# Linformer attention and MLP-mixer on one core: the first batch's loads in another order, and a new written-out order for the opening

## The chip, the cores and the metric

The kernel runs on one core of a Trainium2 chip. The core has a matrix engine (TensorE, "PE" in the profile, with "PEld" for its weight loads), a vector engine (VectorE, "DVE"), a scalar engine (ScalarE, "ACT"), GpSimd ("POOL") and SyncE ("SP"). Each works through its own queue of instructions in order and waits on semaphores for the others. Data is moved by 16 DMA engines, which are fed from queues on SP, ACT and POOL. Matmul results land in PSUM, which has eight banks. The metric is the device time of the whole program in microseconds, the median over runs.

## The reference, cut to what matters

Eight batches; eight heads of 64; a sequence of 1024. First an attention with projected keys and values, then a mixer over tokens and channels:

```python
k_proj = np.einsum('ks,bhsd->bhkd', E, k)          # 1024 -> 64
v_proj = np.einsum('ks,bhsd->bhkd', F, v)
attn = softmax(q @ k_proj.T / 8);  x = attn @ v_proj    # heads side by side: x is (B, 1024, 512)
u = x + (relu(x.T @ w_tok1) @ w_tok2).T            # over tokens, 1024 -> 256 -> 1024
out = u + relu(u @ w_ch1) @ w_ch2                  # over channels, 512 -> 1536 -> 512
```

## The kernel before, in words

The matmuls run in bf16, and the casts from float32 are made by the loads. Batch 0 is a lead-in of its own, the "opening"; from batch 1 on, the attention of the next batch is woven into the channel matmuls of the present one, so that the matrix engine always has channel work (`up_set`, L1180, and `down_block`, L1289, both in a seven-product Strassen form) beside the short attention steps.

In the opening the eight heads are handled as four pairs, 0 to 3 (pair g holds heads 2g and 2g+1). The first batch's q, k and v come as twelve loads of two heads each (`load_heads`, L358), 512 KB in float32 and 256 KB as written. Per pair the steps are:

- `kv_proj` (PE, L521): 16 matmuls that project k and v together. Pair 3 is handled apart: k first, v later, 8 matmuls each. Copies to `kb` and `vb` follow, on ACT or DVE (L334, L336).
- `k_transpose` (PE, L574, one matmul) and a copy to `kT`.
- `q_transpose_pe` (PE, L618, 8 transposes) and a copy of 1024 columns to `qT`.
- `scores` (PE, L637, 4 matmuls into two banks), then two exponentials on ACT (L652) into `a`.
- `attend` (PE, L672): four units of two matmuls; each is followed on DVE by a reciprocal (L686) and a multiplication into `x_sb` (L692), the normalisation.

After that come `token1_part` (PE, L1060: 16 units of four matmuls, which need x of a pair and token weights wt1, in two half loads), `token2_part` (PE, L1092: eight units of eight matmuls, which need wt2; each is followed by an addition into `u` on DVE, L1105), `u_transpose_pe` (PE, L1121: eight units of four, with copies) and then the first channel products. The channel weights are combined on DVE (L476), as are the sums of u (L807).

E and F are transposed on PE in two halves (L462) and copied to `EFT_sb` by ACT and DVE (L465); every `kv_proj` needs both. Ahead of that PE warms up on zeros (L436), and between the early steps it runs "fills": matmuls of 512 columns on zeros whose result nobody reads.

Nothing is scheduled at run time. `Planner.plan` reads the order of all 2204 jobs from the string `ORDER` (two characters per job, a number in base 64, in the order in which the jobs are created) and the PSUM bank of every job that takes one from `SPOTS`. `FILLS` lists the places in that order at which a fill stands ahead of a PE job, once for every fill. An engine's queue holds its jobs in this order, and the loads stand in POOL's queue in it:

```python
for place, j in enumerate(plan):
    if j.eng == "PE":
        for _ in range(FILLS.count(place)):
            blank(zero)
        pin()
```

`LOADS` names the pieces of the first batch, but the order in which they are issued is that of `ORDER`.

Of the kernel before, what the change touches and what calls it, by code (L numbers as in the profile page):

```python
# [12 lines left out]
ACT = mybir.ActivationFunctionType  # L13
EARLY = 12.0
ORDER = (
    "0R000T0Q090P0S0102040W050U0X030V0A1+061-2007240s080v0w0t0u250x0C0z0+0D0y0-111L0B101M1E0E181G1B151C19"
    "1F0H1A1J261I1K1H1D12271N13140G16171P1O0F1W1c1X1Y1T1g1Q1Z1f1e1R1d1S1j0I1U1V1h1k1a1i281b2N0J291l2S1n2O"
    "2T1m0K2P2Q2A1o1u2U1p2R1v1x1r1q3C211s1t2V1y222X232W2Y1w2E1z2H2B2K2F2I2Z2C2a2L2J2l3B2b2D2h2G332M2i2c0M"
    "2d2e342f2p2m2g0L352x2q362t2y2j0O2r2u2k2n372o0Y2-380N2s2v3L302w2z393M0c3D3v0Z2+313I3N3H323d0a3E3O3J3j"
    "3e0d4c0e3P3A3f3Q0f3h0g3g3R9w3F3i0b3S3K3w3-0h3k3T0i3x4Y3l3U3V3y3z3G3m3W3X4a4d5p3Y4Z3+4e3Z6B0j3p4f403q"  # L20
    "5r4g414u4h425A5s3n4v0k4j3o455B4y464k4w4b434z0l4i445E4l4x4m3a4-4n474o3r5q5C4p4B5D0o4+503t4C9v5F495251"
    "4D5H0p5u4J0q5v535w3b5I0m54485x5y555KA15t3c4G5z0n4H565L4q4K3u576D4A4I5+6F4L6E4M3s6C6H6G6O4N6A6P6Q6160"
    "6I9x6R62696L5-4E6J6S6T4O6f6Z6367646g6h4F686a6M6K654s4Q6bA2660r4R4r6N6c6U4P5S6V4S6W4U6d6e4T6Y6i6o6u6X"
    "6j6l6k5T6m6n6r6x6p5U4V6q6s6y6+6z5G6-4W5a705b4X6t5J74717A72736v5M756w77765N785O585Q7B79595c5X7C5R5Y7J"
    "7H7K7F7I7Q7D7G7S7EA55Z7L7R4t5d5PA6A75eA8AA5VA3A45f5W5h5g7M5i7N5lAD5j7O7V5k7Z7W7X7n7a7Y5m7PA97o7d5n7b"
    "7e7T7p7c7r9z7q7g7s7f7hAF7u7iAH7jAG9-7l7U7v7t7mAJ83AI7wAN7x84AOAhAK7zAi7yALAM877kAjAQ857+88Ak8986AP8A"
    "ARASAbAlAm8BAWAcAdAeAX8D8CATAZ8LAfAgENAaAU8F9y8EAEAVB38MAY8GEO8mB4B5AnAt8iAB8n8+AoAz8k8N8oAC7-8q8pAu"
    "5o8T8H8rAv8U818-8jAq8tA+Ap928JAw90A-93Ar8QAs918lB68uAxB095Ay8K9G96B7B18wB8B28s8xB98R9HBBBD988v9K8S99"
    "9IBEBC94EQBF9+EP8yBGBA8W97BI8zBH9A8V9L8X9BBJ9J9NBK9M829OBL8IBN8YBM9QBOA0BV9RBPBR8aBWBSBTBQBk80BYBl8b"
    "BZBaBXBUBcBb8OBd8P9PBfBnBeBp9SBgBhBmBiERBoBjBq8Z9YES9CET9Z9TEWBr9a8e9E8f9UBs9g8cBu9hBt8dC19WEZBzBwC2"  # L30
    "9dB-BxEVC5EU9iC3C69e8gC4C89V8h9DEbC9EYBv9bEdC0Ec9c9FEfEj9fCBEeEgEkElCC9jEhEiEmByB+9kEn9XEpEr9lC7EqCF"
    "CAEo9nCGEsEtCDCHCEEuCI9o9mCJEvEwExCK9rEyEzCXCMCYE+CLCNE-F0CZ9s9pCaCbCO9qF19tCcCdEXCRF2F3F49uCPF5F6Ce"
    "CQEaCpF7CfILFBCSChIMCgCqCiF9CjFCFACrDEFDDADFDCDSFEF8DGDICkDHFGCTDJFFFHClCxDTCVDLFIFLDBFJFMDUFKFPCnDW"
    "DVFQCyDDDXCmFNDMFTFRDKFOFUDOCzCuDPDNFWCvFXDZCwFiDaFaFVFbDQDcFSFcFYDdC+FZFfDkFgFdC-FeFjIPDRFhDlINCUD0"
# [3 lines left out]
    "J9GMHCJAEHEKJ8GPJBGQHQJCELGnGdJ6GbEMJEGeEIJDJFH8GfHRMJHAJJJGGgGhGRMKJKJHHDH9HUGiJIHSGTHEHVHGGjGlJLHH"  # L38
    "JNJRJMGoHTGSJSHiJOHFHJJPJWGpHXJXHKHIHYHBJUGvJVHaHLHMGUJYHNJTHOJZHbGsJQHjHPGtJaHmJbHnJdJcGwJgGxHkHWJe"
    "MNGmJhJfMLGuHZGkJjMRHpHlJkHcHqHoMOGyHrMPJlHdMQJnMSHsMMJoHuHtGzHvGqG+JiHwGrJpH0JmJzG-H1J+HeH+H2J-HyH3"  # L40
    "JqJvH-JrMVJsI0JxH4JtMTK0K1HxH5K2MXH6I6MaHgMbKBHhI7MZJwMYJyK4I8KCI3K5MfMcMgI4MhK7MdMeJuKDK8I5KFMiHfKG"
    "K3MmI9KEK6KIMkHzMnKJIAMoMpMjK9IBKLMqKAKMKHMrIDKKIEMsKTIFI1KUIGMtMlI2MuMvH7KXICKVMUKYMwKNKWQHMxMyKaKZ"
    "KOKbMzIHM+M-LAN3KlLBL6KdL8N0KcLCN1LEN2LDIILFL9N5N7LON6N8KfKeN4N9LPLHKgNBLIL7KmIJNALSKPKnIKNCKhLKQIKi"
    "NDLGLLNEMWLQKRLTNHLJLRNFNIKtKQNGNLKuKjLgKvNJKSNPLVNQNKKqNMLhKkNUNNLWLMNONVLiNSLkQKQJNTKrLNKoLlNWLYNX"
    "KpLZKsNRLjLnNYLmLoNZKwLpNeNbNfLqNcKxLrNaNhLUNdNjLXQLNiKyNgQONlQMK+NmQNLaKzQPK-QQNnLyLbLsL0L2NkL1LzLt"
    "L3QTL+LcNxLuQRNqLvNyNoO9NtL4M4NvM5OAL5LwLeNzOBM6N-OCNuM1NwN+NpM2O0NrO1M3O2ODNsO3QVOEO4O5QZLfM7O6O7QX"
    "OGQWO8M8OHLdOFQYLxQaM9QdL-QbQeOIOJM0QfOKOLQcMBUGOMMCMAUFQlMDQgONMFQjMEQmQhORQnQUMGOSOPQSQoQkP4P8QpQi"
    "QqOTP9OVP6OUOXOOQuOWMHPAOjP7PBMIQvQwOYQrOZPCQsQtQxPDOkOaQ+UHPFQyUIQzOdPGQ-ObR0PMOeOcPIPNOfPeOQOlR5Oh"
    "PQR2POPROrR1PPR3PTR6OoOgPUR4R7PWP5R8OpRAR9RBPSPJRCRFOqOsRGPVRDOtPERERJPYPHRHRNRIOuRORKRLPKPXPZRQPfOv"
    "OiRRRSPiPLRURcPjRVRPUJRWRTRMOwRXUNRZUKPlRYPgRaPmReOyRdPaRbPhPoPcUMPkPpRfPnRhULOzRgUOPwO+PqRiO-RjPxPr"  # L50
    "OmRkPyOnPsRlRmQ2OxQ3PuRnRoP0RpRvPvRqS7Q4RwP1RrRtRxP2P-RyRsP3RzS8RuPbUPR+PdS9UQQ0URS0USQ1SBSASDS1UUSC"
# [8 lines left out]
    "YCYOYRYP"  # L60
)
SPOTS = (
    "1722467307234441203466116170466360762302312744331670103172245374067253415210734175262102125107667450"
    "1520620612306606413423170354767105253604361302764621303237243176464774171176417604252570156254404366"
    "2373521237102235700221317730106123406106503414727325704746701646213666333167646254435756374205316107"
    "3513126156167122221112015160746532017414020057236736457430642470552552655172151277014703436566371016"
    "1004135333425222002277525207405235256117403572635617204"
)
FILLS = (17, 17, 22, 22, 23, 30, 30, 30, 36, 36, 36, 36, 36, 42, 42, 53, 53, 70, 70, 70, 70, 70, 70)
WHOLE = 3  # L70
TWO = 2
T1 = 2
# [115 lines left out]
def kernel(  # L188
# [246 lines left out]
    def blank(z):  # L435
        nc.tensor.matmul(  # L436
            banks[5], z, z[:, None, :].to_broadcast([P, NJ, P]), start=True, stop=True
        )
# [1082 lines left out]
# [4 lines that stand above are left out]
# [40 lines left out]
```

## Time and profile before

| what | value |
|---|---|
| time, median of 3 runs | 418.57 us (417.91 to 418.78) |
| the profiled execution | 419.06 us; its span 417.3 us |
| granted TensorE clock, mean | 0.999 |
| PE busy | 407.7 us, 98% of the span |
| DVE busy | 356.8 us, 85% |
| ACT busy | 221.6 us, 53% |
| DMA | 61.70 MB, mean 148 GB/s |

The 1.76 us between span and time lie around the program. The span counts from the first instruction. The DMA engines are close to full for about the first 75 us: that time holds the weights, the first batch and the loads for the next two.

How the loads of the opening stand before, by slot (the place in POOL's queue), with issue and time to landing from the trace:

| slot | before | issued at | landed after | landed at | in this slot in the changed kernel |
|---|---|---|---|---|---|
| 1 | k of pair 0 | 1.27 | 4.5 | 5.8 | q of pair 1 |
| 2 | k of pair 3 | 3.14 | 4.0 | 7.1 | v of pair 1 |
| 3 | v of pair 0 | 3.87 | 5.9 | 9.8 | k of pair 1 |
| 4 | q of pair 0 | 4.58 | 6.5 | 11.1 | q of pair 2 |
| 5 | v of pair 1 | 5.29 | 7.0 | 12.3 | v of pair 2 |
| 6 | q of pair 1 | 6.00 | 7.6 | 13.6 | k of pair 2 |
| 7 | k of pair 1 | 6.71 | 8.2 | 14.9 | v of pair 0 |
| 8 | q of pair 3 | 7.42 | 8.7 | 16.1 | k of pair 0 |
| 9 | k of pair 2 | 8.13 | 9.3 | 17.4 | q of pair 0 |
| 10 | v of pair 2 | 8.85 | 9.9 | 18.7 | k of pair 3 |
| 11 | q of pair 2 | 10.10 | 10.6 | 20.7 | q of pair 3 |
| 12 | wt1, first half | 11.34 | 10.1 | 21.4 | v of pair 3 |
| 13 | wt1, second half | 12.61 | 10.1 | 22.7 | wt1, first half |
| 14 | v of pair 3 | 13.90 | 10.1 | 24.0 | wt1, second half |
| 15 | wt2 (twice the size) | 15.22 | 11.2 | 26.4 | wt2 |
| 16 to 21 | channel weights w1, six pieces | 16.46 to 22.96 | 11.3 to 11.5 | 27.8 to 34.5 | the same six, in the order of their numbers |

### The profile page before, as it was taken

Reading aid. Unit: us, or ns where it says so; the run is one execution under the profiler, and the core shown is the slowest. Engines: PE = TensorE matmul, PEld = TensorE weight load, DVE = VectorE, ACT = ScalarE, POOL = GpSimd, SP = SyncE. Lnnn points to the kernel's source line nnn. Section 1 sums busy time; section 2 is a strip of 40 time slices with the busy share of each in tenths; the row PEclk is TensorE's granted clock in tenths of the full one; section 3 lists DMA queues with packets and bytes.
Section 4 is the critical chain, followed back from the end, with each engine's and each line's share of the span. In section 5 each row is a group of like instructions: output and inputs, shape, how many; then the busy total and the mean of one; then the engine's idle time right before and its main releaser. Section 6 shows DMA issues by size and latency. Waiting matters only on the chain.

```text
span 417.3 us, 9605 instructions
## 1 busy us (share of the span) xinstructions
PE 407.7 (98%) x3911; PEld 344.6 (83%) x3913; DVE 356.8 (85%) x773; ACT 221.6 (53%) x429; POOL 66.8 (16%) x105
## 2 busy tenths in 40 slices
PE   8999999998999999999999999999999999999995
PEld 4489888687888888989988889888889789988884
DVE  2479899778999999989989898889989899978685
ACT  1658884267536564483654555455644755344340
POOL 8453021012102030101201011023000001010010
PEclk9999999999999999999999999999999999999999
DMA  8999999597998997997958599898984402250134
GB/s 165 206 200 205 207 191 193 154 150 128 202 190 161 158 190 123 198 154 149 210 95 170 106 203 161 155 174 138 226 122 115 101 0 102 52 151 11 43 117 137
DMA packets 93900, 61.70 MB, mean 148 GB/s; under 512 B 59040, under 2 KB 89376, under 8 KB 93856
## 3 DMA queue, kind: packets, MB, share of 16 engines
q0 software_dynamic: 35088, 45.09, 56.0%
q1 hardware_dynamic: 58128, 15.27, 22.1%
q10 hardware_dynamic: 640, 0.72, 0.5%
q8 instruction: 30, 0.49, 0.4%
q14 instruction: 14, 0.11, 0.1%
HBM read 59.24 MB, written 16.78 MB: 182 GB/s over the span
## 4 chain that ended last, share of the span: by engine, by line
PE 82%; DVE 9%; DMA 5%; POOL 1%; issue 1%; SPq 1%; ACT 0%; DVEq 0%; POOLq 0%
PE psum L1289 31%; PE psum L1180 30%; PE psum L991 4%; PE psum L875 4%; PE psum L521 3%; DVE x_sb L692 3%; DMA qT<-q_sb 3%; PE psum L672 3%; DMA k_sb<-in_k_dram 2%; PE psum L637 2%; DVE G L1161 1%; DVE G L1216 1%; PE psum L1092 1%; DVE rdn L686 1%; PE psum L712 1%
## 5 line engine op out<-in xcount | busy, mean ns | idle before, releaser
L1289 PEld LDWEIGHTS <-G 128*128 128x128 bf16 x1356 | 130.0, 98 | 18.0 <-issue 3.1
L1289 PE MATMUL psum<-wc_sb,G 128*128 128x256 bf16 x780 | 101.0, 271 | 0.0
L1180 PEld LDWEIGHTS <-wc_sb 128*128 128x128 bf16 x768 | 73.9, 98 | 9.5 <-issue 1.4
L1289 PE MATMUL psum<-wT,G 128*128 128x256 bf16 x576 | 76.1, 273 | 0.0
L1202 ACT ACTIVATE G<-psum 128x512 bf16<-128x512 f32 x96 | 56.4, 601 | 28.4 <-PE psum L1180 27.8
L1216 DVE TENSOR_TENSOR G<-G 128x512 bf16<-128x512 bf16 (+1 forms) x140 | 68.8, 515 | 0.4
L1180 PEld LDWEIGHTS <-wT 128*128 128x128 bf16 x576 | 55.4, 98 | 8.5 <-issue 1.9
L1180 PE MATMUL psum<-S,wT 128*128 128x256 bf16 x384 | 56.7, 273 | 0.0
L1327 POOL DMA_DIRECT2D out_dram<-o x30 | 16.4, 547 | 250.5 <-DVE o L1336 183.8
L1180 PE MATMUL psum<-S,wc_sb 128*128 128x256 bf16 x384 | 56.3, 273 | 0.0
L1180 PE MATMUL psum<-uT,wc_sb 128*128 128x256 bf16 x384 | 56.1, 273 | 0.0
L692 DVE TENSOR_TENSOR x_sb<-psum,rdn 128x256 bf16<-128x256 f32 (+1 forms) x88 | 46.9, 542 | 2.1
L1336 DVE TENSOR_TENSOR o<-psum,u 128x512 f32<-128x512 f32 x59 | 40.3, 684 | 7.4 <-PE psum L1289 6.5
L1223 ACT COPY psum<-psum 128x512 f32<-128x512 f32 x48 | 27.7, 579 | 27.1 <-PE psum L1180 18.4
L1161 DVE CUSTOM_DVE_ANT_0 G<-psum,ua 128x512 bf16<-128x512 f32 x48 | 32.6, 683 | 7.4 <-ACT ua L1208 4.0
L652 ACT ACTIVATE a<-psum 128x512 bf16<-128x512 f32 x64 | 34.6, 605 | 8.2 <-PE psum L637 8.2
L1208 ACT COPY ub<-psum 128x512 f32<-128x512 f32 x48 | 28.3, 589 | 19.1 <-PE psum L1180 11.3
L1208 ACT COPY ua<-psum 128x512 f32<-128x512 f32 x48 | 28.2, 592 | 17.5 <-PE psum L1180 17.4
L1161 DVE CUSTOM_DVE_ANT_0 G<-psum,ub 128x512 bf16<-128x512 f32 x48 | 32.8, 684 | 2.8 <-PE psum L1180 2.5
L1180 PE MATMUL psum<-uT,wT 128*128 128x256 bf16 x192 | 28.8, 273 | 0.1
L672 PE MATMUL psum<-vb,a 128*128 128x130 bf16 x256 | 25.0, 220 | 0.2
L686 DVE RECIPROCAL rdn<-psum 128x4 f32<-128x4 f32 (+1 forms) x88 | 15.3, 184 | 9.9 <-PE psum L672 9.2
(102 smaller groups left out, 497.8 us busy)
## 6 DMA issues: line engine op xcount, KB each, us to landing
out_dram<-o POOLq DMA_DIRECT2D x30, 512.0 KB, 4.5
v_sb<-in_v_dram POOLq DMA_DIRECT2D x14, 512.0 KB, 8.0
k_sb<-in_k_dram POOLq DMA_DIRECT2D x14, 512.0 KB, 10.2
q_sb<-in_q_dram POOLq DMA_DIRECT2D x14, 512.0 KB, 9.3
wc_sb<-in_moe_w_ch_dram POOLq DMA_DIRECT2D x6, 256.0 KB, 11.4
wc_sb<-in_moe_w_ch_dram POOLq DMA_DIRECT2D x4, 384.0 KB, 14.3
k_sb<-in_k_dram POOLq DMA_DIRECT2D x4, 256.0 KB, 6.4
v_sb<-in_v_dram POOLq DMA_DIRECT2D x4, 256.0 KB, 8.5
```

The lines of the kernel that those rows point to most:

```text
L652: lambda g=g, half=half, bk=bk: nc.scalar.activation(out=a_t[g][:, half], in_=bank(bk), func=ACT.Exp, scale=scale),
L672: nc.tensor.matmul(view()[:, k, c].rearrange("p i d -> p (i d)"), a_t[g][:, c, at : at + P], vb[:, g].rearrange("k i d -> k (i d)"), start ...
L686: lambda: nc.vector.reciprocal(out=rdn, in_=view()[:, :, :, :, D]),
L692: lambda: nc.vector.tensor_tensor(out=x_sb[:, rows, g * P : (g + 1) * P].rearrange("p (n c) (i d) -> p n c i d", c=2, i=2), in0=view()[:, ...
L1161: nc.vector._custom_dve(TENSOR_ADD_SAT, out=out, in0=in0, in1=in1, s0=FMAX, s1=0.0)
L1180: nc.tensor.matmul(t[:, c, :], w1_of(n, dd, 2 * m + c), a_of(j, n, dd), start=(n in (1, 7) and c == 0 and dd == 0), stop=(c == 1 and dd == 1),
L1202: lambda: nc.scalar.activation(out=G[:, n, cs], in_=view(src), func=ACT.Relu),
L1208: 512, lambda: nc.scalar.copy(out=dst, in_=view("y")), writes=[(name, s % 2)],
L1216: 512 * len(both), lambda: f(out=G[:, n, c], in0=G[:, a, c], in1=G[:, b, c]), ps=False,
L1223: 512, lambda: nc.scalar.copy(out=view("y"), in_=view("x")), takes=[bk["y"]],
L1289: nc.tensor.matmul(to, G[:, G_OF[n], cc, t * P : (t + 1) * P], w2_of(n, cc)[:, cut], start=(n in opens and (t == 0 or alone) and cc == 0), ...
L1336: 512, lambda: nc.vector.tensor_add(out=dst, in0=view(src), in1=u_of(sh, dh)),
```

## The change

Three constants differ, `ORDER`, `SPOTS` and `FILLS`; no function does. The diff, cut:

```diff
 ORDER = (
-    "0R000T0Q090P0S0102040W050U0X030V0A1+061-2007240s080v0w0t0u250x0C0z0+0D0y0-111L0B101M1E0E181G1B151C19"
+    "0R050T0Q040P0S0308070U061L0V0W01000X021M091E0A1F1G1I1H1J0B1K1N1j1O0C1P1W1X1Y1c0D1e1f1g1d1k1Q0E1h1Z1i"
...
-FILLS = (17, 17, 22, 22, 23, 30, 30, 30, 36, 36, 36, 36, 36, 42, 42, 53, 53, 70, 70, 70, 70, 70, 70)
+FILLS = (21, 21, 21, 21, 21, 21, 21, 27, 27, 30, 35, 35, 45, 45, 45, 53, 53, 68, 68, 80, 80)
```

Decoded, it does this:

- The loads change places as the last column above shows: pair 1, pair 2, pair 0, pair 3, and only then the token weights. The w1 pieces (and the four w2 pieces further on) go in the order of their numbers.
- PE's first 101 jobs are reordered. Up to the first token products the order is (with n fills as "[n]"; "kv" is `kv_proj`, "kT" and "qT" the transposes of k and q, "S" the scores, "A" one unit of attend, "T" half of the transposes of E and F; the digit is the pair):

```
before: T T [2] k3 [2] kT3 [1] kv0 [3] kT0 qT0 [5] S0 qT1 [2] kv1 A0 A0 A0 [2] kT1 qT3 A0 S1 [6] A1 kv2 A1 A1 A1 qT2 kT2 S3 token1 ... S2 ... A2 ... v3 ... A3
after:  T qT1 T [7] kv1 [2] kT1 [1] S1 qT2 [2] A1 kv2 [3] A1 kT2 A1 [2] kv0 S2 kT0 qT0 A1 [2] k3 S0 kT3 [2] qT3 A0 A0 A0 A0 v3 S3 A2 A2 token1 ... A2 A2 A3 ...
```

- There are 21 fills where there were 23.
- ACT's and DVE's queues follow: in the changed kernel ACT's is kT1, two exponentials of pair 1, four copies of kv2, qT2, two kb copies of pair 0, an exponential of pair 2, two vb copies, kT0, qT0, the other exponential of pair 2, two of pair 0, kT3, qT3, two of pair 3. On DVE the 16 normalisations still stand ahead of the first addition into u, in the new order of the pairs; the sums for w1 and u (L476, L807) are interleaved otherwise behind them, and the first of the sums of the token weights (L830) stands later.
- Behind PE's first 101 jobs, ACT's first 64 and DVE's first 87 (they end among the first channel products of batch 0) each engine's own order of compute jobs is the same as before. Behind that, one load differs: the first half of v for batch 2 moves from ahead of batch 2's q to behind the second half of v. In later batches six results go to another PSUM bank.

## The prediction

> **What bounds the kernel now.** First the page, then the opening in windows, in order of time engine by engine, and in the chain of waits.
>
> ```profile
> PE 407.7 (98%) x3911; PEld 344.6 (83%) x3913; DVE 356.8 (85%) x773; ACT 221.6 (53%) x429; POOL 66.8 (16%) x105
> PEclk9999999999999999999999999999999999999999
> ```
>
> PE works nearly all the time, so the end moves only if PE waits or fills less, and that it does, almost alone, in the opening. The windows (busy us of each engine, clock, DMA share):
>
> ```profile
> 15.00:20.00 5.00, 4.83 (x63) 2.76 (x62) 3.53 (x15) 2.28 (x5) 2.96 (x4) 1.00 1.22 208
> 20.00:25.00 5.00, 4.51 (x67) 3.43 (x62) 2.48 (x11) 4.30 (x10) 2.69 (x4) 1.00 1.15 207
> 25.00:30.00 5.00, 4.95 (x79) 4.56 (x79) 4.89 (x19) 0.77 (x2) 2.33 (x4) 1.00 1.44 198
> 30.00:35.00 5.00, 5.00 (x81) 4.91 (x80) 4.87 (x10) 3.87 (x8) 2.52 (x4) 1.00 1.38 200
> ```
>
> Up to 25 PE's time holds waits and fills (the fills count as busy) and DVE is half idle; the loads set the pace. From 25 on PE and DVE are both full. The rows of PE and DVE around that turn:
>
> ```profile
> 24.88 0.63 PE L521 MATMUL psum<-v_sb,EFT_sb 128*64 128x128 bf16 x8
> 25.45 0.84 PE L1060 MATMUL psum<-x_sb,wt_sb 128*128 128x128 bf16 x12
> 26.34 0.72 PE L672 MATMUL psum<-vb,a 128*128 128x130 bf16 x8
> ...
> 24.50 0.25 DVE L686 RECIPROCAL rdn<-psum 128x4 f32<-128x4 f32 x2 [2.19 <-PE psum L672]
> 27.29 1.40 DVE L692 TENSOR_TENSOR x_sb<-psum,rdn 128x256 bf16<-128x256 f32 x4
> 28.67 3.90 DVE L1105 TENSOR_TENSOR u<-psum,x_sb 128x512 bf16<-128x512 f32 x6
> ```
>
> Pair 3's v, landed at 24.0 in slot 14, is projected at 24.88; its attend is at 26.34, and DVE, idle for 2.19 us before 24.50, normalises pairs 2 and 3 until 28.67. The rest runs without a gap: in the chain the next batch's first projection is "41.72 0.99 PE psum L521 x16". My mark for comparison is 35.01, when all of the opening and two groups of channel products are done. One stall is left later:
>
> ```profile
> PE psum L637 <- DMA qT<-q_sb: 1.2, 1, 1.2
> ```
>
> That one, at 98, hangs on transposes which SP issues after a projection at 79.02, so it moves along with PE.
>
> **The loads.** Every load of the first batch has one size, so I take the landings by slot as they were (5.8, 7.1, 9.8, then about 1.3 apart). The DMA share stays the same, and POOL's queue holds the same number of loads ahead of each slot. Three things follow: all q, k and v are there at 21.4 instead of 24.0; wt1 comes one slot later (22.7 and 24.0); wt2 (26.4) and w1 don't move.
>
> **The new order, walked.** Durations from rows of before: a projection takes 0.57 on PE (14.97 to 15.54); its four copies on ACT 0.98 (10.49 to 11.47); a qT copy 1.01, the next starts after 0.91; from the first score matmul to the first exponential 0.46; two exponentials 1.08; a kT copy 0.27; an attend unit 0.13; a token1 unit 0.225; a token2 unit 0.50 (three from 27.46 to 28.96). Start and warm-up stay, with PE free for T at 5.56.
>
> - Pair 1: T, qT1, T end at 7.4, seven fills at 8.9, and k in slot 3 (9.8) starts kv1 at 9.85: PE idles 1.0. DVE's kb copies end at 11.07, kT at 11.67, S1 is at 11.73, exponentials until 13.27.
> - Pair 2: k (slot 6, 13.6) gives kv2 at 13.68, ACT's copies 14.3 to 15.3, qT2 until 16.3.
> - Pair 0: k (slot 8, 16.1) gives kv0 at 16.2. From here ACT's queue is the path: kb until 17.4, exponential of pair 2, vb until 18.3, kT0, qT0 until 19.5, exponential of pair 2, S0 at 19.6, two exponentials until 21.15, kT3 until 21.4, qT3 until 22.4.
> - Pair 3: q in slot 11 (20.7) is turned by 21.4, before ACT is free; v (21.4) is projected from 21.7. S3 is at 22.5, exponentials from 22.95 to 24.04.
>
> Before, pair 3's exponentials shared ACT's 2.19 us block after 22.35; what held pair 3 back was v. So 2.6 us of earlier data become little here: ACT's queue, not the load, is late next.
>
> **PE's sum.** Before, from 24.88 to the mark: 10.13 us. After, PE is past S3 at 22.83; against before at 24.88 it has v3 done (less 0.57) but 7 more token1 units (7 x 0.225 = 1.58) and 4 more attend units (0.52) to do: 11.66, so the mark at 34.5, 0.5 earlier. In that stretch PE needs wt1 at 23.1 (landed 22.7, 24.0) and wt2 at 27.8 (26.4): covered by 0.4 to 1.4 us; if a load is later than that, it counts in full.
>
> **DVE's sum.** From the first normalisation of pair 0 (21.54), DVE has 12 units and two vb copies (0.50). A unit by itself takes 0.55 (20.73 to 21.28); reciprocals side by side bring it to 0.43 (four in 26.99 to 28.69). With the queue's actual pairs I get the end at 28.15 against 28.67. PE waits for single units on the way (the last four attend units and token1 of pairs 2 and 3), 0.3 in all beyond what before has. So 0.5 less 0.3: the mark is 0.2 to 0.3 earlier, and I take 0.3. Bounds: with every unit at 0.43 DVE ends at 27.2, no wait is left and PE can also win back the 0.5 of waits that before has in this stretch, together 1.1 earlier; with each unit at 0.57 and PE waiting for all of it, 0.3 later.
>
> **The rest.** Two fills fewer are 2 x 0.22 of PE time, at places where PE waits anyway: nothing. Token and channel sums on DVE stay as many. SP's queue is unchanged. The half v of batch 2 used to be issued at 43.02 (landed 60.0) and now stands among the loads at 59.65 to 64.06, of which the last landed at 74.1; with 2.6 us more that is under 77, and its reader starts at 79.02: nothing, and beyond that cover one for one. PE found no gap in front of any of the six results that get other banks: nothing. First users of batch 1's loads at 41.72 had them from 39.6: 2.1 us of cover, enough for 1.1.
>
> **A rule.** The granted clock is 1.00 in every window and a 512-column fill takes 0.22 us. The changed order leaves PE 1.0 idle at 8.9 and about a quarter of 10 to 22.5. [...]
>
> **Sum.** 419.06 of the profiled execution less 0.3 is 418.8; that execution was 0.5 above the median, so the median goes from 418.57 to 418.3. About 0.2% (0.84 us) is what can be told from no change.
>
> **Rivals.**
> 1. Faster: DVE pairs its reciprocals better and PE loses the waits. 0.9 to 1.1 earlier: 417.5. For it: DVE has all attend results of pair 2 early, and idles today before 24.50. Against: the queue's order alternates reciprocals and multiplications.
> 2. Slower: the chain through ACT slips. Pair 0's k sits in slot 8 and the eight jobs behind it on ACT all wait in line; one slot (1.28 us) later there, or as much lost between PE and ACT by in-order waiting, passes whole to qT3, S3 and PE: 1.28 less 0.3 is 1.0, so 419.6. It decides from 0.3 on. For it: ACT has no slack from 16.8 to 24, where before it was busy 2.28 of 5 us in 15 to 20. Against: landings by slot have one cause and didn't depend on the tensor.
> 3. Slower: batch 2's late half v delays the transposes behind 79 and the stall at 98 grows by 1.5: 419.8. Against: 2 us or more of cover.
> 4. Slower: the clock falls once. At half clock the PE work of pair 1's stretch (0.57 + 0.23 + 0.34 + 0.45) takes that much again, 1.6: 419.9. Against: 1.00 throughout, and no gap over 1.0.
>
> **How the numbers follow.** Forecast 0.46, rival 1 0.25, rival 2 0.21, rival 3 0.05, rival 4 0.03. Faster by over 0.2% (below 417.7) is rival 1: 0.25; slower (above 419.4) are 2 to 4: 0.29, less 0.01 for small slips: 0.28; within: 0.47. The range from 417.4 to 419.6 leaves out rivals 3 and 4 and the tails of 1 and 2; the forecast's own is 417.9 to 418.9.
>
> **What would show it.** In the changed trace: kv1 at 9.85; v of pair 3 landed by 21.5; S3 near 22.5 and straight behind qT3's copy; DVE without a gap from 21.5 and at its first addition into u at 28.2; token2's first matmul near 27.8; batch 1's first projection at 41.4; the stall at 98 of the same size; clock 1.00. The prediction is wrong if S3 comes after 23 (rival 2), if additions into u start before 27.5 (rival 1), or if PE has a new gap behind 42.

## The result, and the profile after

| | before | changed |
|---|---|---|
| median of 6 runs each | 418.3 us (417.91 to 418.78) | 419.82 us (419.64 to 421.2) |
| profiled execution | 419.06, span 417.3 | 419.9, span 418.1 |

The ratio is 1.0044 (95% interval 1.0030 to 1.0058): slower, by 1.5 us between the medians, where 0.2% can be told from no change. A second comparison, on another chip and with 12 runs of the changed kernel beside 35 of before, gave 1.0024 (1.0014 to 1.0033), which is 1.1 us between the medians. The forecast was 418.3, 0.3 faster; its range ended at 419.6.

The page of the changed kernel, and then its windows of the opening, in the columns of the prediction:

```profile
PE 406.9 (97%) x3911; PEld 344.5 (82%) x3911; DVE 357.0 (85%) x773; ACT 221.2 (53%) x429; POOL 66.8 (16%) x105
PEclk9999999999999999999999999999999999999998
```

```profile
15.00:20.00 5.00, 4.10 (x50) 2.44 (x49) 1.39 (x6) 4.22 (x12) 2.80 (x4) 1.00 1.24 206
20.00:25.00 5.00, 4.49 (x56) 3.14 (x56) 3.44 (x16) 3.81 (x7) 2.38 (x4) 1.00 1.14 210
25.00:30.00 5.00, 4.92 (x80) 4.55 (x78) 4.60 (x17) 1.05 (x3) 2.23 (x3) 1.00 1.41 195
30.00:35.00 5.00, 5.00 (x81) 4.91 (x79) 4.91 (x10) 3.83 (x8) 2.97 (x4) 1.00 1.39 201
```

PE works less between 15 and 20 (4.10 for 4.83), DVE more between 20 and 25 (3.44 for 2.48), and the clock stays at 1.00. The rows around the turn from waiting to full engines, PE first, then DVE, from the timeline:

```profile
21.47 0.62 PE L618 MATMUL psum<-ident,q_sb 128*128 128x128 bf16 x8 [0.31 <-DMA q_sb<-in_q_dram]
22.48 0.63 PE L521 MATMUL psum<-v_sb,EFT_sb 128*64 128x128 bf16 x8
23.19 0.41 PE L637 MATMUL psum<-qT,kT 64*64 64x512 bf16 x4
...
28.27 0.76 DVE L692 TENSOR_TENSOR x_sb<-psum,rdn 128x256 bf16<-128x256 f32 x2
29.23 1.29 DVE L1105 TENSOR_TENSOR u<-psum,x_sb 128x512 bf16<-128x512 f32 x2 [0.20 <-PE psum L1092]
```

Pair 3's scores come at 23.19 (forecast 22.5), 1.1 us behind the end of a q transpose that waited for its load; the normalisation ends at 29.03 (before 28.69, forecast 28.15), and the first addition into u starts at 29.23 (before 28.67). A group of channel products of batch 1 (L1289) serves as a later mark, from here on "the mark at 87.4"; it is the last that I compare ahead of the stall near 98 us. Its row in before, then in the changed kernel:

```profile
87.20 0.82 PE L1289 MATMUL psum<-wT,G 128*128 128x256 bf16 x6
```

```profile
87.73 0.82 PE L1289 MATMUL psum<-wT,G 128*128 128x256 bf16 x6
```

Against the first trace of before, PE is 0.53 us late at the mark and 0.77 late at its end (413.04 for 412.27), so something is lost twice. One late wait of PE grew, the one near 98 us, which was 1.2 us:

```profile
PE psum L637 <- DMA qT<-q_sb: 1.5, 1, 1.5
```

### The profile page after: what moved, and what is told of

It reads as the page before. It is cut to its first block, busy times and chain, and to the rows that moved or that the text cites. A ratio compares the mean times of both kernels' runs of the same rounds, so it can differ in the third digit from the quotient of the medians.

```text
span 418.1 us, 9597 instructions
## 1 busy us (share of the span) xinstructions
PE 406.9 (97%) x3911; PEld 344.5 (82%) x3911; DVE 357.0 (85%) x773; ACT 221.2 (53%) x429; POOL 66.8 (16%) x105
## 4 chain that ended last, share of the span: by engine, by line
PE 82%; DVE 7%; DMA 6%; POOL 2%; issue 1%; SPq 1%; ACT 0%; POOLq 0%; DVEq 0%
PE psum L1289 31%; PE psum L1180 30%; PE psum L991 4%; PE psum L875 4%; PE psum L521 3%; DMA qT<-q_sb 3%; DMA q_sb<-in_q_dram 3%; DVE x_sb L692 3%; PE psum L672 2%; PE psum L637 2%; DVE G L1216 1%; PE psum L1092 1%; DVE G L1161 1%; PE psum L712 1%; PE psum L1060 1%
## 5 line engine op out<-in xcount | busy, mean ns | idle before, releaser
L1289 PEld LDWEIGHTS <-G 128*128 128x128 bf16 x1356 | 130.0, 98 | 18.0 <-issue 3.1
L1289 PE MATMUL psum<-wc_sb,G 128*128 128x256 bf16 x780 | 101.0, 271 | 0.0
L1289 PE MATMUL psum<-wT,G 128*128 128x256 bf16 x576 | 76.1, 273 | 0.0
## 6 DMA issues: line engine op xcount, KB each, us to landing
wc_sb<-in_moe_w_ch_dram POOLq DMA_DIRECT2D x6, 256.0 KB, 11.6
```

Source lines behind the costliest of these rows:

```text
L1289: nc.tensor.matmul(to, G[:, G_OF[n], cc, t * P : (t + 1) * P], w2_of(n, cc)[:, cut], start=(n in opens and (t == 0 or alone) and cc == 0), ...
```

## The experiments

All landings below are from the issue rows of the traces, PE's times from its matmul rows; the mark is the start of the first matmul of its group. Two sums hold in all 17 traces, whatever the order, and make them easy to compare. The mark comes 58.49 to 58.55 us behind the first addition into u. And PE's end comes 323.83 to 323.96 us behind the mark, plus PE's waits in between (the one near 98 us, and 0.22 us near 101 in two traces). So a difference between two traces is either there by the first addition into u, in the opening, or it arises in these waits.

### Both kernels again, and the half load of batch 2

The first edit moves one job in the order before, the second moves the same job back in the changed order (loads of batch 2 in POOL's queue; v0 is the half with heads 0 to 3, v1 the other half, and so for q and k):

```diff
 # the order before, decoded             # the changed order, decoded
-v0 q0 v1 k1 k0 q1                       -q0 v1 v0 k1 k0 q1
+q0 v1 v0 k1 k0 q1                       +v0 q0 v1 k1 k0 q1
```

> The kernel before, unchanged, as a control and for a second trace of it. The medians of the two kernels lie 1.5 us apart (418.3 and 419.8), their two traces only 0.85 (spans 417.3 and 418.1): the profiled execution of before, 419.06, was 0.76 above its own median. Theory 1 (the trace of before caught a late execution, and the change costs 1.5 us in places that this trace hid): the new span is 416.4 to 416.8, and something in it lies 0.5 us or more earlier than in the first trace. Theory 2 (executions scatter by that much and the change costs about what the traces show, 0.5 in the opening and 0.25 at the stall near 98 us): the new span is again near 417. In the time of other runs: the same within 0.1%.

> The changed kernel, unchanged, on the same chip, as the other control. 1.0036 times before if the first comparison holds (1.5 us; interval 1.003 to 1.006). If the loads of the opening land late by a property of the order, q of pair 3 lands again between 21.3 and 21.5 us and the fourth load at 11.4; if it was an accident of that execution, they land as in the trace of before, at 20.7 and 11.05, and the difference to before shrinks by about 0.5 us.

> The kernel before with one job moved: the first half of v for batch 2 goes from ahead of q of batch 2 to behind the second half of v, where the changed kernel has it. Theory 'stall': the second q transpose of batch 2 lands about 0.25 us later, the stall of the matrix engine near 98 us grows by 0.2 to 0.3, and the time grows by 0.2 to 0.3 us (ratio 1.0005 to 1.0008). Rival 'the half load is inert': 0 and no growth of the stall; then the 0.23 us by which the stall grew came with the later opening. Rival 'queue': a transfer behind it is pushed and the loss is 0.5 or more.

> The changed kernel with that one half load of batch 2 back where the kernel before has it. Theory 'stall': 0.2 to 0.3 us faster than the changed kernel (419.5 for 419.8), with the stall near 98 us back at its size before. Rival 'inert': the same time as the changed kernel.

Measured, on one chip, with before at 418.74 (35 runs): before again 418.68, ratio 1.0005 (0.9994 to 1.0016); changed again 419.88, 1.0024 (1.0014 to 1.0033); before with the half load late 419.03, 1.0004 (0.9993 to 1.0014); changed with it early 419.92, 1.0026 (1.0015 to 1.0036). The half load is inert: neither time moved, and the stall did not go back.

The two controls say more, from their timelines near 98 us, before first, then changed:

```profile
96.78 0.28 PE L672 MATMUL psum<-vb,a 128*128 128x130 bf16 x2
97.81 0.63 PE L637 MATMUL psum<-qT,kT 64*64 64x512 bf16 x8 [0.75 <-DMA qT<-q_sb]
```

```profile
96.77 0.28 PE L672 MATMUL psum<-vb,a 128*128 128x130 bf16 x2
98.45 0.63 PE L637 MATMUL psum<-qT,kT 64*64 64x512 bf16 x8 [1.40 <-DMA qT<-q_sb]
```

PE arrives within 0.01 us of the same time (at the mark, 87.39 and 87.38) and then waits 0.75 in the one and 1.40 in the other, for the second q transpose of batch 2 (a DMA that SP issues). It ends at 411.98 and 412.63: all of PE's 0.65 arises in this one wait. In the chain of work that ended last the transpose is a piece by itself (start and length), 11.93 us in before and 12.64 in changed:

```profile
85.84 11.93 DMA qT<-q_sb
```

```profile
85.76 12.64 DMA qT<-q_sb
```

So the opening's loss in the first pair of traces, 0.53 at the mark, is for the greater part an accident of that execution: the fourth load landed at 11.44 there, at 10.91 and 10.59 in the two new traces of the changed order, and the mark followed (87.73, 87.38, 87.09). The second trace of before has the mark 0.19 later than the first (87.39 for 87.20) and PE's end 0.29 earlier, since its stall is 0.48 shorter. The spans of the controls are 0.8 us apart and their medians 1.2 (0.8 by their ratios to before, 1.0005 and 1.0024); what the one pair of traces doesn't show of that stays open here.

### Take the stall away, and three rivals for the opening and the code

```diff
 # both orders, decoded, POOL's queue; store3 is the third store of batch 0's output
-v(batch 3, first half)  store3  q(batch 3, first half)
+v(batch 3, first half)  q(batch 3, first half)  store3
```

> The kernel before with one store moved: the third store of an output half of batch 0, issued at 86.6 us between the two batches' transfers, goes in the POOL queue behind batch 3's load of q, which can't start before the second q transpose of batch 2 has landed. The store's 128 packets take 1.3 us of all 16 DMA engines, inside the time in which that transpose runs. Theory 'stall' (the scores of pairs 2 and 3 near 98 us wait for that landing alone, 0.7 to 1.2 us in the order before): the landing comes about 1.3 us earlier, the wait nearly vanishes, and the kernel gets 0.7 to 1.1 us faster (ratio 0.9974 to 0.9983). Rival 'opening' (the time is set in the opening, the stall moves along): no gain over 0.2 us.

> The changed kernel with the same store moved. Theory 'stall': its wait near 98 us (1.4 to 1.7 us) vanishes as well, it gets 1.2 to 1.6 us faster than the changed kernel, and its matrix engine ends within 0.35 us of the kernel before with the store moved, because the two openings are equal at 87.4 us in the pair of traces taken on one chip. Ratio to before 0.997 to 0.999. Rival 'opening': it stays 0.6 us or more behind the kernel before with the store moved.

Measured, with before at 418.56 on that chip: before with the store moved 417.9, ratio 0.9986 (0.9977 to 0.9996); changed with the store moved 418.42, 0.9998 (0.9987 to 1.0008), where the changed kernel stands at 1.0024. The second transpose landed 10.5 and 10.7 us behind the issue of batch 3's v, for 12.4 and 13.0, and neither trace has a wait for qT on PE; its ends are 410.85 and 411.54. The stall theory holds in kind: 0.6 us gained in the order before, 1.1 in the new one, each a little less than was expected (0.7 to 1.1 and 1.2 to 1.6). The two ends lie 0.69 apart, where at most 0.35 was expected. Of that 0.49 stood at the mark already (86.94 and 87.43), and 0.22 is a new wait near 101 in the changed order. In these two executions the fourth load landed at 10.43 and 11.13. Whether the opening costs something is open here.

The next edit pads DVE's code ahead of everything else, on the changed kernel:

```diff
+    spare = tile_of([P, 8], BF16, "spare")
+    for _ in range(7):
+        nc.vector.memset(spare, 0.0)
```

> The changed kernel with seven writes of zeros into 8 columns that nobody reads, on DVE ahead of everything else, where DVE is idle. The new opening order needs seven semaphore instructions fewer on DVE (910 instructions for 917), so everything behind it stands seven places earlier in DVE's code; the traces show a code fetch for a queue that is not PE's at 90.1 to 90.5 us in the order before and at 87.3 to 88.0 in the new one, and DMA packets stuck near 91 us for 0.5 to 1.3 us a DMA engine before, 2.9 to 3.1 after. Theory 'code position': the fetch goes back to about 90, the stuck time falls to 1.3 or less, the second q transpose lands at 97.8 to 98.0 instead of 98.4 to 98.8, and the time is 0.5 us or more below the changed kernel. Rival 'code does not matter': landing at 98.4 or later and the time of the changed kernel, 1.0024 times before.

Measured: 1.0026 (1.0015 to 1.0037), landing 13.4 us behind, PE's wait 1.8 us, the code fetch at 87.86, within the range without the padding (87.33 to 87.97). The length of DVE's code makes no difference here.

The third edit of this group takes the copy of pair 0's qT from ACT to DVE (one letter of the string that says which engine makes each copy):

```diff
-SIDES = "AAADADADADDAAAAAAAAADAAAAAAAA"
+SIDES = "AADDADADADDAAAAAAAAADAAAAAAAA"
```

> The changed kernel with the copy of pair 0's transposed q on DVE instead of ACT. The prediction made ACT's queue the path of the opening; the three traces of the new order have the scores of pair 3 exactly 1.76 us behind the landing of q of pair 3 (21.43, 21.07, 20.76 to 23.19, 22.83, 22.52). Theory 'landing': that distance stays at 1.7 to 1.8 us, the first additions into u stay where they were against that landing, and the time stays within 0.2 us of the changed kernel. Rival 'ACT': ACT is 1.0 us of work shorter ahead of the scores of pair 3, the distance falls by 0.3 us or more, and the first channel products come 0.3 us or more earlier.

Measured: 1.0027 (1.0017 to 1.0036) for the changed kernel's 1.0024, so no gain. The rows (ACT, then PE) show why:

```profile
20.56 0.27 ACT L336 CAST kT<-psum 128x128 bf16<-128x128 f32 x1
21.64 1.01 ACT L336 COPY qT<-psum 128x1024 bf16<-128x1024 bf16 x1 [0.81 <-PE psum L618]
...
20.98 0.62 PE L618 MATMUL psum<-ident,q_sb 128*128 128x128 bf16 x8 [0.44 <-DMA q_sb<-in_q_dram]
22.75 0.41 PE L637 MATMUL psum<-qT,kT 64*64 64x512 bf16 x4
```

ACT is free 0.81 us before it can copy pair 3's qT (0.41 in the changed kernel), and the scores stay 1.82 us behind the landing of q of pair 3 (20.93). The load sets them here, not ACT's queue.

### One POOL instruction

The DMA engines also bring code: the pages of both kernels have two queues of the kind "instruction", q8 (30 packets, 0.49 MB) and q14 (14 packets, 0.11 MB). With the store moved, the fetch of q14 that is near 88 or 90 us in the other traces was at neither place (100.13 and 100.42). That pointed at POOL, which is then held up behind batch 3's load. POOL's code has 175 instructions in the order before and 176 in the new one (174 and 175 of them are in the traces): ahead of the first q load of batch 1 stands a semaphore instruction that the order before doesn't have, since the load there has one thing to wait for (a DMA) and here two (a DMA and PE). It stands at 33.84 in the first changed trace; both orders have one ahead of the first v load of batch 1 (24.02 and 24.70), which waits for two as well. The first edit below adds an instruction to the kernel before, behind that same q load (the trace has it at 34.51); the second takes one from the changed kernel, a clearing in the opening that isn't needed. Both diffs are cut:

```diff
         j.fn()
+        if j.n == 205:                      # behind the first q load of batch 1
+            nc.gpsimd.memset(spare, 0.0)
```

```diff
-        make_identity(nc, ident32)
+        nc.gpsimd.affine_select(out=ident32, in_=zero32, compare_op=ALU.not_equal,
+                                fill=1.0, base=0, pattern=[[-1, P]], channel_multiplier=1)
```

> The kernel before with one instruction more on POOL: a write of zeros into 8 columns that nobody reads, behind the last load of k for batch 1, so that POOL's code has 176 instructions as in the changed kernel (one semaphore instruction more) and not 175. In the traces the code fetch that is not PE's comes at 90.1 to 90.5 us in the order before, at 87.3 to 88.0 in the new one, and with the store moved, POOL being held up behind batch 3's load, it is at neither place in either order: so it is POOL's. Padding DVE's code left it at 87.9. Theory 'POOL code': the fetch comes at 87.2 to 88.0, the first q transpose of batch 2 takes 4.6 us for 4.41, packets near 91 us are stuck for 2.8 us or more for 0.6 to 1.4, the second transpose lands 13.0 to 13.4 us behind the issue of batch 3's v for 12.4 to 12.9, and the kernel is 0.4 to 0.7 us slower than before (ratio 1.001 to 1.0017). Rival 'another trait of the new order': fetch at 87.6, but landing and time as before (1.000).

> The changed kernel with one instruction less on POOL: the float identity is made from zeros that DVE has already written, so one clearing of 128x128 goes. POOL's code has 175 instructions as before. The loads behind it may be issued up to 0.2 us earlier. Theory 'POOL code': the fetch is back at 90.1 to 90.5 us, the first q transpose takes 4.41, the second lands 12.4 to 12.9 us behind the issue of batch 3's v, stuck packets 0.6 to 1.4 us, and the time is 0.4 to 0.7 us below the changed kernel: ratio to before 1.000 to 1.0015 for 1.0024. Rival 'another trait': landing 13.0 or more behind, ratio 1.002 or more, less what the earlier loads give.

Measured, with before at 418.82: the kernel before with one instruction more 419.85, ratio 1.0017 (1.0009 to 1.0026); the changed kernel with one less 419.06, 1.0001 (0.9990 to 1.0011). Both times lie in the range that was expected, at its upper and its lower end. Three of the signs do not: with one more, 2.0 us of packets are stuck (see the table) where 2.8 or more was expected; with one less, 0.3 are stuck for 0.6 to 1.4, and the transpose lands 12.0 us behind batch 3's v for 12.4 to 12.9. The chain's piece for the second transpose, before with one more, then changed with one less:

```profile
85.60 12.63 DMA qT<-q_sb
```

```profile
85.71 11.58 DMA qT<-q_sb
```

And the fetch, from the DMA view of two stretches: 87.0 to 88.5 us in the control of the changed kernel and in before with one instruction more (both have it there; the control of before has no such line), and 89.9 to 92.9 in the control of before and in changed with one less (queue, then packets, MB and share of the DMA engines' time):

```profile
q14 instruction: 1, 0.01, 1.3%
```

```profile
q14 instruction: 1, 0.01, 1.3%
```

```profile
q14 instruction: 1, 0.01, 1.9%
```

```profile
q14 instruction: 1, 0.01, 1.6%
```

All traces up to here. "Stuck" is the length of the DMA packets that took over 0.4 us and began between 89.8 and 93.5, summed and divided by the 16 DMA engines (the median packet of a load takes 0.1):

| kernel | POOL's fetch | first q transpose | second lands, behind the issue of batch 3's v | stuck | PE's wait near 98 | mark at 87.4 | PE's end |
|---|---|---|---|---|---|---|---|
| before, first trace | 90.31 | 4.41 | 12.85 | 1.4 | 1.2 | 87.20 | 412.27 |
| before, control | 90.54 | 4.41 | 12.38 | 0.6 | 0.7 | 87.39 | 411.98 |
| before, half load late | 90.15 | 4.41 | 12.69 | 1.3 | 1.1 | 87.24 | 412.14 |
| changed, one POOL instruction less | 90.28 | 4.42 | 12.00 | 0.3 | 0.4 | 87.26 | 411.53 |
| before, one POOL instruction more | 87.41 | 5.07 | 13.07 | 2.0 | 1.4 | 87.15 | 412.48 |
| changed, first trace | 87.97 | 4.58 | 13.09 | 3.1 | 1.5 | 87.73 | 413.04 |
| changed, control | 87.64 | 4.62 | 13.02 | 2.9 | 1.4 | 87.38 | 412.63 |
| changed, half load early | 87.33 | 4.61 | 13.31 | 3.0 | 1.7 | 87.09 | 412.62 |
| changed, DVE padded | 87.86 | 4.63 | 13.38 | 3.4 | 1.8 | 87.59 | 413.20 |
| changed, qT of pair 0 on DVE | 87.50 | 4.62 | 13.15 | 3.3 | 1.5 | 87.24 | 412.62 |
| before, store moved | 100.13 | 4.41 | 10.52 | 1.6 | none | 86.94 | 410.85 |
| changed, store moved | 100.42 | 4.43 | 10.67 | 1.7 | none | 87.43 | 411.54 |

Fetch near 90: 12.0 to 12.9 us to the landing. Fetch near 87.5, while the first transpose is in flight: 13.0 to 13.4, without overlap, and the first transpose takes 0.2 to 0.7 longer. One POOL instruction moves it either way. That the fetch is the link, and not something else that the instruction shifts, is concluded from this match alone. The second edit also issues the loads of the opening 0.18 earlier, but its mark (87.26) isn't early; its gain is in the wait, 0.4 for 1.4 to 1.8. That is less than before's 0.7 to 1.2, so the equal time (1.0001) doesn't say that the changed opening is free. In the other direction the wait accounts for part: 1.4 for 0.7 to 1.2, and PE ends 0.2 to 0.5 later than in the three other traces with this order and the store in its place, while the time is 0.7 longer. How a fetch of 8 KB that lasts 0.31 us does this is not shown: the stuck packets are a sign of it and not the whole of it, since with the store moved 1.6 us are stuck and nobody is late.

### No fills

```diff
-FILLS = (21, 21, 21, 21, 21, 21, 21, 27, 27, 30, 35, 35, 45, 45, 45, 53, 53, 68, 68, 80, 80)
+FILLS = ()
```

> The changed kernel without its 21 fills. Theory 'landing' (the opening goes by the landing of q of pair 3): the scores of pair 3 stay 1.7 to 1.8 us behind that landing, the granted clock stays at 1.00 and the time within 0.3 us of the changed kernel. Rival 'clock' (the prediction's fourth): the matrix engine is idle for about 40% of 9 to 22 us instead of a quarter, the granted clock falls in a window before 25 us, matmuls there take up to twice as long, and the kernel is 1 us or more slower.

Measured (4 runs): 421.83, ratio 1.0063 (1.0047 to 1.0079), 1.6 us above the changed kernel's 1.0024. The rival 'clock' holds. Windows (clock third from the right):

```profile
8.00:12.00 4.00, 1.56 (x23) 0.83 (x23) 1.36 (x5) 0.28 (x2) 2.99 (x5) 0.87 1.09 173
12.00:16.00 4.00, 2.60 (x29) 2.13 (x29) 0.61 (x2) 2.28 (x7) 1.86 (x4) 0.50 1.24 205
16.00:20.00 4.00, 3.78 (x40) 2.76 (x38) 1.21 (x5) 2.76 (x8) 2.25 (x3) 0.50 1.24 205
20.00:24.00 4.00, 3.56 (x40) 2.22 (x38) 2.18 (x9) 3.31 (x6) 1.72 (x3) 0.85 1.15 213
```

The granted clock halves at about 11 and comes back at about 21: by windows of 1 us it is 1.00 up to 10, 0.97 from 10 to 11, 0.50 from 11 to 21, 0.91 from 21 to 22 and 1.00 again from 22. Eight transposes take 1.03 us there for 0.62, and pair 3's scores come at 23.72 though its q had landed at 20.08.

### The opening by itself, and a kernel faster than both

The store moved and POOL's clearing of the float identity dropped, in both orders; and in the order before, a third edit:

```diff
 # the order before, decoded, loads in slots 12 to 14
-wt1(first half) wt1(second half) v3
+v3 wt1(first half) wt1(second half)
```

> The kernel before with the store moved as in the earlier run and the float identity made from the zeros that are there. If the opening goes by the landing of its loads and these are issued 0.1 to 0.2 us earlier, it gains as much over the moved store alone: ratio to before 0.9978 to 0.9986, no wait near 98 us. If POOL's clearing was hidden, the same as the moved store alone, 0.9986.

> The kernel before with the same two edits, beside the last one on one chip. 0.9986 times before, as it was, no wait near 98 us; this is the kernel that the two others of this call are compared with.

> The changed kernel with the store moved and the float identity made from the zeros that are there: the wait near 98 us is gone and POOL's code fetch lies near 100 us, as in the kernel before with the same two edits, so that only the openings differ. Theory 'opening neutral' (the whole loss came through the stall): within 0.1% of that kernel, and its matrix engine within 0.3 us at 87.4 us. Rival 'opening costs half' (the two kernels with the moved store lay 0.12% apart, 0.5 us of which stood at 87.4 us already): 0.4 to 0.6 us behind it, ratio to before 0.9995 to 1.0005.

> The kernel before with the same two edits and one part of the change: v of pair 3 ahead of the two halves of the token weights wt1, so that these stand behind all twelve loads; PE's order stays. In the traces of before the first token product starts 0.9 to 1.4 us behind the landing of wt1's first half in slot 12, which now comes in slot 13, 1.25 us later. Theory 'wt1 bounds': the first token product comes 0.3 to 0.9 us later and the kernel is 0.3 to 0.9 us slower than with the two edits alone. Rival 'hidden' (the normalisation on DVE sets when the additions into u start, and PE catches up): the first channel products come at the same time, and the time is the same within 0.2 us.

Measured: the order before with both edits 418.18, 0.9986 (0.9977 to 0.9995), and on another chip, beside the next two, 418.06, 0.9981 (0.9971 to 0.9991); the changed order with both 418.43, 0.9990 (0.9980 to 1.0001); the order before with both and the token weights behind all twelve loads 418.95, 1.0007 (0.9992 to 1.0023). PE at the mark: 86.39 and 86.70 in the order before, 87.08 in the changed one, 87.97 with the late token weights. None of the four has a wait for qT.

So the changed opening alone is 0.4 us behind (0.9990 to 0.9981), and 0.5 in the pair with the moved store; the intervals overlap in both pairs, and the control pair had 0.0 at the mark. The mean mark over the five traces of each order with the opening's POOL work and copies as they were is 87.18 before and 87.44 changed, 0.26 later, in a spread of 0.45 and 0.64. I leave it at 0 to 0.5. With the 0.65 of the stall in the controls that gives an estimate of 0.65 to 1.15 us for the whole change, beside 0.8 to 1.2 measured there.

The order before with only the token weights moved behind loses 1.1 us. Its first product with them, in the order before with both edits and then with the late token weights:

```profile
21.68 0.40 PE L1063 MATMUL psum<-x_sb,wt_sb 128*128 128x128 bf16 x4
```

```profile
22.95 0.40 PE L1063 MATMUL psum<-x_sb,wt_sb 128*128 128x128 bf16 x4 [0.54 <-DMA wt_sb<-in_moe_w_tok_dram]
```

That is 1.27 later, and the mark moves by the same 1.27. Half of it is the execution (fourth load at 11.28 for 10.61), the rest the wait for the later slot, inside the 0.3 to 0.9 expected. The 0.9 to 1.4 us from landing to first product that the expectation starts from don't hold for the first product: it follows by 0.04 to 0.67 in the five traces of before's opening, so the token weights nearly bind there already. Dropping POOL's clearing issues the loads from slot 2 on 0.18 earlier, and PE ends 0.2 to 0.5 earlier in the traces; the times don't settle whether that is a gain (0.9986 and 0.9981 for 0.9986 in the order before, 0.9990 for 0.9998 in the changed one).

The order before with the store moved is faster than the kernel before by 0.14% (0.14% and 0.19% with POOL's clearing dropped too), and so faster than the changed kernel: the one long wait that PE had behind the opening is gone.

## Why the prediction was wrong, point by point

Two steps failed: a stall that was taken to move along grew, and the 0.3 us that the opening was to gain didn't come. The first is shown; of the second the size stays open.

- **"That one, at 98, hangs on transposes which SP issues after a projection at 79.02, so it moves along with PE."** This step failed. The issue does move along with PE; the time from there to the landing was taken as fixed. Counted from the issue of batch 3's v, it was 13.0 to 13.4 us for 12.4 to 12.9 in every trace of the changed order with the extra POOL instruction and the store in its place. That makes PE's wait 1.40 for 0.75 us, which is all of PE's difference in the pair of controls. Removing one POOL instruction takes the wait to 0.4 and the time to 1.0001.
- **"POOL's queue holds the same number of loads ahead of each slot"** is right, and misses what mattered: its code isn't the same length. I counted the loads in each queue and not the semaphore instructions that come with them.
- **Rival 3** had the right place (the stall at 98 grows), but the wrong cause, and its time, 419.8, is right by luck: the stall grew by 0.2 and 0.65 in the two pairs, not by 1.5. Moving the half load back changed nothing. As "The rest" had it, that load costs nothing.
- **"The loads": "I take the landings by slot as they were".** As a mean, right up to slot 10, where the means of the two orders agree within 0.09; from slot 11 on they don't. The fourth load landed at 11.05, 11.04, 11.06, 10.43 and 10.93 in orders before, at 11.44, 10.91, 10.59, 11.13, 11.02 and 10.82 in changed ones. As single values they scatter by up to 0.85 us between executions of one order, and slot 12's 21.43, on which the walk leaned, was the earliest of its kind (21.75 to 22.12 in the four others). Slot 11, on which pair 3's scores hang, landed at 20.51 to 20.94 in five traces of before's opening (mean 20.74) and at 20.76 to 21.43 in six of the changed one (mean 21.09), though at 20.08 in the one without fills; why it comes later isn't shown. A margin of 0.4 us against a load is none.
- **"The new order, walked": "From here ACT's queue is the path".** Wrong wherever q of pair 3 lands behind 20.7: then the scores are 1.76 to 1.82 us behind that landing in seven traces, with or without 1.0 us of work taken off ACT (20.7 is an estimate: 22.47, the earliest scores of the changed order, less 1.76). With its q at 20.76 they come at 22.52, where I had 22.5. With its q at 20.00 (changed order, both edits) they come at 22.47, no earlier: there the chain runs through the load of k of pair 3, in slot 10, and DVE's copies of it.
- **"DVE's sum"** was 0.35 short: from the scores of pair 3 to the first addition into u it is 6.03 to 6.07 us in seven traces with the copies as in the changed kernel and its fills, for 5.7 in my walk; DVE's alternating reciprocals and multiplications take 0.55 a unit in most of that stretch, where I had 0.43 to 0.57 mixed. With slot 11's 0.35 that is the whole miss: the first addition into u comes at 28.92 in the mean of five traces, for 28.2 forecast and 28.66 in before. The 0.3 of further PE waits that I put on top aren't there, since the mark at 87.4 keeps its distance to that addition in both orders.
- **The forecast of "0.3 earlier"** at the end of the opening, from "PE's sum" and "DVE's sum", is the second step that failed. At the mark the changed order is 0.53 later (first pair), 0.01 earlier (controls), 0.15 earlier (the two with the half load moved), 0.49 later (store moved) and 0.38 later (both edits, on one chip). By the mean it is later, and how much of that is the order and how much the landings of single executions isn't settled. The stall hides it in part: with the mark 0.29 earlier than in the control (half load early) the transpose landed at the same 98.41.
- **"A rule": "The granted clock is 1.00 in every window".** It stayed at 1.00 in the changed kernel too, in every window of its trace up to 50 us. That it would, with no gap over 1.0, was my estimate. The fourth rival's fall is real without the fills: the granted clock is 0.50 from 11 to 21 us, where eight transposes take 1.03 us for 0.62. Ahead of that PE's longest gap was 2.3 us, and between 7 and 11 it was busy for 0.88 of 4 us, where the changed kernel with its fills has 3.41 at 1.00. So the 21 fills are worth 1.6 us, though no result of theirs is used. How long a gap, or how little work, brings the clock down is not shown.

## What to carry to other kernels

Before a late stall is said to move along, look at what else runs while the awaited transfer is in flight: a wait on a DMA need not keep step with the engine that waits (here 0.75 and 1.40 us, with PE at the same place within 0.01). A reordering can also change which instructions need an extra wait, so the code's length changes, and with it the times at which code is fetched (here 176 POOL instructions for 175, and a fetch at 87.64 for 90.54 in the controls); compare the number of instructions of each engine, not only the jobs. And take a second trace of the same kernel before giving a landing to a tenth of a microsecond: the fourth load of the changed order landed between 10.59 and 11.44.

## What the runs showed of the hardware that was not expected

- Code is fetched by the DMA engines all through the run: one queue brings 30 fetches of 16 KB (q8, 18.7 to 399.7 us in the first trace of before), another 14 of 8 KB (q14, 33.2 to 413.7). One POOL instruction more or less, which moves a fetch of 8 KB by 3 us (90.54 to 87.41, 87.64 to 90.28), goes with about 0.2% of the kernel's time (1.0017 for 1.0000 in the order before, 1.0024 for 1.0001 in the new one).
- The first q transpose of batch 2 lands 4.41 us behind its issue (4.6 to 5.1 with the fetch near 87.5). The second, of the same size and issued behind it beside a load and a store, lands 11.6 to 13.0 us behind its own; with the store moved, 10.1 to 10.6.
- After the fills were taken out, the granted clock, 0.50 from 11 us on, needed until 21 us to return, with PE busy for 3.78 of the 4 us from 16 to 20.
